# Channel attention then GLU on one core: first chunk's weights kept on chip, half of one batch's squares formed later, v's sums made by accumulating DMA

## The chip, the cores and the metric

The kernel runs on one core of one Trainium2 chip. The metric is the device time of one execution in microseconds, as the median of several runs. The engines named below are PE (matmuls), PEld (its weight loads), DVE (vector), ACT (scalar), POOL (GpSimd, here almost only the issuer of accumulating DMAs) and SP (the issuer of nearly all other DMAs).

## The reference, cut to what matters

Four batches (B = 4) of N = 6080 tokens with C = 256 channels pass through attention over channels and then through a gated layer. `q`, `k`, `v` are float32, the two weight matrices are float64.

```python
qn = q / (np.linalg.norm(q, axis=1, keepdims=True) + 1e-06)
kn = k / (np.linalg.norm(k, axis=1, keepdims=True) + 1e-06)
s = kn.transpose(0, 2, 1) @ qn / tau          # 256 x 256 for each batch
s = s - s.max(-1, keepdims=True)
a = np.exp(s)
a /= a.sum(-1, keepdims=True) + 1e-09
x = v @ a                                     # tokens x 256
h = x @ w_in                                  # d_ff = 2048
g = h * (1.0 / (1.0 + np.exp(-1.702 * h)))
out = g @ w_out
```

## The kernel before, in words

The attention matrix of a batch is multiplied into `w_in` once (`weights`, 8 units of 256 columns of d_ff each), so that the main part works straight on `v`: `g(v @ (a @ w_in)) @ w_out`. Both products of the main part are done by a 2x2 Strassen scheme with seven products (M1 to M7), in float32r with a high and a low part: three matmuls for one product (`three`).

The main part goes over the batches, in each over six chunks of 1024 tokens (the last has 960), in each over eight **pairs** (one unit of `w_in` and `w_out`). `front` forms the gated hidden values of a pair, `back` multiplies them with `w_out`. A pair's place counts from 0 over the whole program, 48 places to a batch. A chunk needs seven high-low tiles of `v` or of sums of its blocks; `values` makes them, in the order M5, M1, M2, M6, M7, M3, M4. Four of them need sums, which DVE adds in the kernel before.

What comes ahead for each batch:

- `Attention.unit`: scores (k transposed times q, summed over the tokens) from two row tiles at a time, 24 units to a batch, the last of 64 rows; and the squares of q and k for the norms: ACT squares, the sum goes into `acc`. For batches one and two (`b` = 0 and 1) the scores are float32 matmuls straight from the staged rows (`ps_s<-raw`), and DVE adds the squares. The rows come by `load_direct`, 1 MB (q and k) to a load, into staging buffers that are used again in turn. For batches three and four the rows are loaded unit by unit, split in high and low (`hl`), and an accumulating DMA from POOL (`acc<-raw`) adds the squares.
- `Attention.finish`, the softmax: column sums of `acc` (`ps_n`), roots on POOL (`rn`), scales spread by PE (`ps_b`), maximum and exponential, a transpose (`ps_t`), high and low part (`aT`).
- `weights`: the product `ps_w`, its Strassen sums (`wf`), high and low parts (`w`, stored in `w_d` for the later chunks).

The float64 weights are converted from their 32-bit words in the program: `win_convert` (loads `words<-in_w_in`, result stored in `win_d`) and `wout_convert` (`words<-in_w_out`, result with its sums stored in `wout_d`). In the kernel before, the first chunk reads both back from there: `wi<-win_d`, `wo<-wout_d`.

Each operation is a node with an engine, a cost, a due time and dependencies; a planner orders all nodes and the program is issued in this order. So every engine, and SP's and POOL's queues too, works through a fixed list in order, and an instruction that waits holds up all that stand behind it on its engine. The table that places the work ahead is `{1: (0, 6), 2: (19, 60), 3: (74, 118)}`: the scores of batch `b` are planned between these places (for batch two they come before place 0 already), the softmax from `end + 1`, the weights from `end + 4`, one unit to a place.

Of the kernel before, what the change touches and what calls it, by code (L numbers as in the profile page):

```python
# [20 lines left out]
P = 128  # L21
# [19 lines left out]
class Node:  # L41
    __slots__ = ("eng", "cost", "lag", "fn", "deps", "uses", "due", "idx", "start", "left", "ready", "outs")

    def __init__(self, eng, cost, fn, deps, uses, due, lag, idx):
        self.eng, self.cost, self.fn, self.due, self.lag, self.idx = eng, cost, fn, due, lag, idx
        self.deps = [d for d in deps if d is not None]
        self.uses = list(uses)
        self.start = None


class Plan:
# [27 lines left out]
    def graph(self):  # L79

        nodes = list(self.nodes)
        free_of = {}
        for n in self.nodes:
            deps = {id(d): d for d in n.deps}
            for b in n.uses:
                prev = b.prev
                while prev is not None and not prev.users:
                    prev = prev.prev
                if prev is not None:
                    r = free_of.get(id(prev))  # L90
                    if r is None:
                        r = Node(None, 0, None, prev.users, (), 0, 0, len(nodes))
                        free_of[id(prev)] = r
                        nodes.append(r)
                    deps[id(r)] = r
            n.deps = list(deps.values())
        ins, outs = [[] for _ in nodes], [[] for _ in nodes]
        for n in nodes:
            for d in n.deps:
                w = d.cost + d.lag  # L100
                if n.eng is not None and n.eng != d.eng:
                    w += self.DRAIN.get(d.eng, 0) + self.HOP + self.MARGIN.get(n.eng, 0)
                ins[n.idx].append((d.idx, w))
                outs[d.idx].append((n.idx, w))
        return nodes, ins, outs

# [84 lines left out]

VSUM = lambda b, c: False
QSUM = lambda b: b >= 2
HIACT = True
TURNED = True
TAILX = True
STQ = False
# [20 lines left out]
def channel_attention_then_glu(  # L218
# [61 lines left out]
    win_d = dr.tile([NPAIR, P, 2, NC2, 2 * P], F32, name="win_d")  # L280
    wout_d = dr.tile([NPAIR, P, 2, NA + 1, P], F32, name="wout_d")
    w_d = [dr.tile([NPAIR, P, 2, NA - 1, P], F32, name=f"w_d{i}") for i in range(B)]
# [141 lines left out]

    win_ready = {}

    def win_convert(grp, c, due, slot, lows, after=()):
# [7 lines left out]
        h = cast(lambda: hl()[:, 0], lambda: wf(), 4 * P, [n], [wf, hl], due + 0.7)  # L435
        l = low(lambda: hl()[:, 1], lambda: wf(), lambda: hl()[:, 0], 4 * P, [h], [wf, hl], due + 0.8)
        st = [
            load(
                lambda a=a: win_d[2 * grp + a, :, :, c, :],
                lambda a=a: hl()[:, :, a * 2 * P : (a + 1) * 2 * P], 256, [l], [hl], due + 1,  # L440
            )
            for a in range(2)
        ]
        for a in range(2):
            win_ready.setdefault(2 * grp + a, []).append(st[a])

    wout_ready = {}

    def wout_convert(u, due, slot, lows, after=()):
        raw = sbuf(slot, [P, 2, C, 2], U32, "words")  # L450
# [9 lines left out]
        h = cast(lambda: st()[:, 0], lambda: f(), 8 * P, [n], [f, st], due + 1)  # L460
        l = low(lambda: st()[:, 1], lambda: f(), lambda: st()[:, 0], 8 * P, [h], [f, st], due + 1.1)
        wout_ready[u] = load(lambda: wout_d[u], lambda: st(), 1024, [l], [st], due + 1.2)


    class Attention:
# [39 lines left out]
        def unit(self, u, due, after=()):  # L505
# [37 lines left out]
            for j in range(nt):  # L543
# [24 lines left out]
                news.append(n)  # L568
            if u == 0:
                self.acc_n = [g.add(  # L570
# [21 lines left out]
            else:  # L592
# [7 lines left out]
                    )  # L600
                ]

        def finish(self, slot):
# [128 lines left out]
    def weights(at, u, due, after=(), slot="Z", kept=None):  # L732

        wi = sbuf("wi", [P, 2, NC2, 2 * P], F32R, "wi")
        r = load(lambda: wi(), lambda: win_d[u], 512, [*win_ready[u], *after], [wi], due - 10)
        pb = bank(slot, "w")

        def fn():
            for i in range(NC2):
                ci = slice(i * P, (i + 1) * P)  # L740
                n = 0
                for l, m in ((0, 0), (0, 1), (1, 0)):
                    for j in range(NC2):
                        nc.tensor.matmul(  # L744
                            pb()[:, i * 2 * P : (i + 1) * 2 * P], lhsT=at.aT()[:, l, j, ci], rhs=wi()[:, m, j, :],
                            start=i == 0 and n == 0, stop=True, skip_group_check=True,
                        )
                        n += 1

        n = g.add("PE", 1440, fn, [at.a_h, at.a_l, r], [at.aT, wi, pb], due)  # L750
        f = sbuf(f"ra{u % 2}", [P, 8, P], F32, "wf")
# [368 lines left out]
    def fetch_wo(ck, p, u, due, after=()):  # L1120
        is_s = ck.kinds[p][2]
        cut = slice(1, 1 + NI) if is_s else slice(0, 4)

        def make(i):
            w = sbuf(f"wo{i}", [P, 2, NI, P], F32R, "wo")
            n = load(
                lambda: w()[:, :, : cut.stop - cut.start], lambda: wout_d[u, :, :, cut, :], 640,
                [wout_ready[u], *after], [w], due,
            )
            return w, n  # L1130

        return wo_slots.get((u, is_s), make)

    held = [None, {}]

    def fetch_wb(ck, p, pairs_of, due, after=()):
# [9 lines left out]
        if u not in places:  # L1146
            i = len(places)
            n = load(
                lambda: w()[:, i], lambda: wout_d[u, :, :, 1 + NI :, :], 256, [wout_ready[u], *after], [w], due,
            )  # L1150
            places[u] = n, i
# [32 lines left out]
    for u in range(2):  # L1184
        wout_convert(u, -55 + 4 * u, f"gi{u}", "oc1")
    nxt = Attention(1)
# [5 lines left out]
    for u in range(nu):  # L1192
        nxt.unit(u, -40 + 4.5 * u)


# [16 lines left out]
    def softmax_at(b, i):  # L1212
# [6 lines left out]
        return fn  # L1219

    def weights_at(b, u):
        return lambda t, here: weights(attention[b], u, t + 4, here)

    for b, (begin, end) in {1: (0, 6), 2: (19, 60), 3: (74, 118)}.items():
        if b >= 2:
            for u in range(nu):
                plan(begin + int(u * (end - begin) / nu), scores_at(b, u))
        for i in range(3):
# [6 lines left out]
    for b in range(B):  # L1235
        for s in range(total):
# [56 lines left out]
```

## Time and profile before

| | before |
|---|---|
| median of 3 runs | 2083.2 us (2081.8 to 2083.36) |
| profiled execution, its own time | 2082.57 us |
| its span, first to last instruction | 2080.8 us |
| PE busy | 2055.2 us (99%) |
| DVE busy | 1970.5 us (95%) |
| ACT busy | 1730.1 us (83%) |
| POOL busy | 110.6 us (5%) |
| DMA | 457.76 MB, mean 220 GB/s |
| mean granted TensorE clock | 0.999 of full speed |

The time stands 1.8 us over the span of the same execution, and the median of the runs 0.6 us over that execution's time. Busy time of PE counts a matmul from its start to its modelled end, so that a stretch in which matmuls follow closely is fully busy. The trace writes a float32 matmul of the direct scores as two records (`x8` for the four matmuls of a pair of row tiles).

### The profile page before, as it was taken

How to read it: one execution, taken by the hardware profiler on the slowest of the kernel's cores; microseconds unless marked ns; L12 is line 12 of the kernel's file. 1: busy time of each engine (PE TensorE's matmuls, PEld its weight loads, DVE VectorE, ACT ScalarE, POOL GpSimd, SP SyncE). 2: the span in 40 equal slices, each digit the busy share in tenths (PEclk: the TensorE clock that was granted, in tenths of full speed). 3: DMA queues.
4: the chain of work that ended last, by engine and by line, in shares of the span. 5: the costliest groups of instructions: out<-in, count | busy, mean ns of one | idle time of the engine just before them, and what ended most of it. 6: DMA issues, size and time to landing. Idle time of an engine off the chain costs nothing.

```text
span 2080.8 us, 27525 instructions
## 1 busy us (share of the span) xinstructions
PE 2055.2 (99%) x9556; PEld 1716.9 (83%) x9556; DVE 1970.5 (95%) x2457; ACT 1730.1 (83%) x2505; POOL 110.6 (5%) x127
## 2 busy tenths in 40 slices
PE   9899999999999999999999999999999999999999
PEld 8788888888888888888888888878888888888887
DVE  8997999999999999999999999999999999999898
ACT  6677888888888888888888888888888788888786
POOL 0000000010110100000000000010000000000000
PEclk9999999999999999999999999999999999999999
DMA  9986877778787666786777867648557555545545
GB/s 361 372 311 233 284 251 243 216 199 252 196 263 233 174 196 230 243 262 190 212 224 220 260 198 202 196 153 301 204 175 229 179 167 162 197 154 165 192 145 156
DMA packets 200314, 457.76 MB, mean 220 GB/s; under 512 B 17520, under 2 KB 87408, under 8 KB 199152
## 3 DMA queue, kind: packets, MB, share of 16 engines
q1 hardware_dynamic: 183072, 414.25, 57.2%
q0 software_dynamic: 17104, 41.75, 11.2%
q8 instruction: 76, 1.25, 0.2%
q14 instruction: 62, 0.51, 0.1%
HBM read 347.34 MB, written 66.85 MB: 199 GB/s over the span
## 4 chain that ended last, share of the span: by engine, by line
PE 74%; DVE 15%; ACT 4%; DMA 3%; issue 3%; SPq 0%; POOL 0%; DVEq 0%; ACTq 0%
PE ps_o L875 20%; PE ps_X L875 15%; PE ps_k L875 14%; PE ps_Z L875 10%; PE ps_Y L875 10%; DVE gp L312 3%; PE ps_s L558 3%; DVE gi L333 2%; DVE ga L312 2%; PE ps_w L744 2%; DVE acc L312 1%; DVE gr L333 1%; DVE gj L333 1%; DMA raw<-in_k 1%; ACT ga L902 1%
## 5 line engine op out<-in xcount | busy, mean ns | idle before, releaser
L875 PE MATMUL ps_X<-v,w 128*128 128x512 f32 (+1 forms) x1728 | 485.7, 389 | 2.1 <-ACT ps_Z L304 1.6
L875 PEld LDWEIGHTS ps_X<-v,w 128*128 128x128 f32 x1728 | 320.6, 188 | 70.3 <-ACT ps_Z L304 5.1
L333 DVE TENSOR_TENSOR gi<-ga,gi 128x1536 fp32r<-128x1536 f32 (+2 forms) x192 | 329.5, 1716 | 12.8 <-ACT gi L304 12.5
L902 ACT ACTIVATE ga<-ga 128x512 f32<-128x512 f32 (+1 forms) x384 | 238.7, 628 | 110.4 <-DVE ga L312 108.7
L875 PE MATMUL ps_Y<-v,w 128*128 128x512 f32 (+1 forms) x1152 | 324.7, 390 | 1.6 <-ACT ps_Y L304 1.6
L875 PE MATMUL ps_Z<-v,w 128*128 128x512 f32 (+1 forms) x1152 | 324.0, 389 | 1.0 <-ACT wf L304 0.5
L875 PE MATMUL ps_o<-gi,wo 128*128 128x512 f32 (+1 forms) x1200 | 322.4, 388 | 1.0 <-DVE oc L318 1.0
L875 PE MATMUL ps_o<-gj,wo 128*128 128x512 f32 (+1 forms) x1152 | 314.2, 388 | 1.5 <-DVE oc L312 1.0
L875 PE MATMUL ps_k<-gr,wb 128*128 128x512 f32 (+1 forms) x1104 | 293.2, 388 | 0.0
L304 ACT CAST gi<-ga 128x1536 fp32r<-128x1536 f32 (+2 forms) x192 | 279.1, 1454 | 4.7 <-PE ps_k L875 1.9
L875 PEld LDWEIGHTS ps_o<-gi,wo 128*128 128x128 f32 x1200 | 224.7, 188 | 47.1 <-DVE oc L318 1.8
L875 PEld LDWEIGHTS ps_Z<-v,w 128*128 128x128 f32 x1152 | 215.5, 188 | 46.3 <-ACT ps_Z L304 1.0
L875 PEld LDWEIGHTS ps_o<-gj,wo 128*128 128x128 f32 x1152 | 215.4, 188 | 45.1 <-DVE oc L312 1.4
L875 PEld LDWEIGHTS ps_Y<-v,w 128*128 128x128 f32 x1152 | 213.3, 188 | 47.5 <-ACT ps_Y L304 6.2
L875 PEld LDWEIGHTS ps_k<-gr,wb 128*128 128x128 f32 x1104 | 206.6, 188 | 41.0 <-DVE kb L312 0.2
L312 DVE TENSOR_TENSOR gp<-ga 128x1024 f32<-128x1024 f32 (+1 forms) x184 | 222.8, 1211 | 16.0 <-ACT ga L902 12.9
L333 DVE TENSOR_TENSOR gr<-gp,gr 128x1024 fp32r<-128x1024 f32 (+1 forms) x184 | 222.6, 1210 | 16.1 <-ACT gr L304 16.0
L333 DVE TENSOR_TENSOR gj<-gp,gj 128x1024 fp32r<-128x1024 f32 (+1 forms) x184 | 222.6, 1210 | 11.7 <-ACT gj L304 10.9
L304 ACT CAST gr<-gp 128x1024 fp32r<-128x1024 f32 (+1 forms) x184 | 191.5, 1041 | 30.1 <-DVE gp L312 27.5
L304 ACT CAST gj<-gp 128x1024 fp32r<-128x1024 f32 (+1 forms) x184 | 191.5, 1040 | 18.6 <-DVE gp L312 16.1
L875 PE MATMUL ps_k<-gi,wo 128*128 128x512 f32 (+1 forms) x552 | 155.0, 389 | 0.5 <-DMA wo<-wout_d 0.2
L304 ACT COPY ps_Y<-ps_X 128x512 f32<-128x512 f32 (+1 forms) x192 | 110.8, 577 | 31.3 <-PE ps_X L875 29.9
(127 smaller groups left out, 2721.6 us busy)
## 6 DMA issues: line engine op xcount, KB each, us to landing
w<-w_d SPq DMA_DIRECT2D x144, 768.0 KB, 5.0
wo<-wout_d SPq DMA_DIRECT2D x118, 640.0 KB, 5.2
wb<-wout_d SPq DMA_DIRECT2D x129, 256.0 KB, 4.1
acc<-raw POOLq DMA_DIRECT2D x44, 512.0 KB, 6.3
v_raw<-in_vT SPq DMA_DIRECT2D x20, 1024.0 KB, 7.7
out_T<-oc SPq DMA_DIRECT2D x80, 256.0 KB, 3.0
w<-w_d SPq DMA_DIRECT2D x144, 128.0 KB, 4.1
w_d<-wst SPq DMA_DIRECT2D x24, 768.0 KB, 5.2
```

Of the source, the lines that this page charges most:

```text
L304: return g.add("ACT", act(n, psum), lambda: nc.scalar.copy(dst(), src()), deps, uses, due)
L312: return g.add("DVE", dve(n), lambda: nc.vector.tensor_tensor(dst(), a(), b(), op=op), deps, uses, due)
L333: lambda: nc.vector.tensor_tensor(dst(), src(), hi().bitcast(F32), op=ALU.subtract),
L558: nc.tensor.matmul(out, lhsT=hl()[:pp, 1, j, l, ci], rhs=hl()[:pp, 0, j, r, :], start=begin and m == 0, stop=True, skip_group_check=True,)
L744: nc.tensor.matmul(pb()[:, i * 2 * P : (i + 1) * 2 * P], lhsT=at.aT()[:, l, j, ci], rhs=wi()[:, m, j, :], start=i == 0 and n == 0, stop=Tr ...
L875: nc.tensor.matmul(dst, lhsT=l(a), rhs=r(b), start=begin and n == 0, stop=True, skip_group_check=True,)
L902: lambda: nc.scalar.activation(dst(), src(), AF.Gelu_apprx_sigmoid, scale=sign), deps, uses, at,
```

## The change

Four things change, and with them the whole order that the planner makes.

- **First chunk's weights.** `win_convert` keeps both halves of a group (two units) in one `hl` buffer, and the first chunk's `ps_w` reads them there; `wi<-win_d` is gone for the first chunk, the store to `win_d` stays. `wout_convert` forms the four plain blocks of `w_out` right in the `wo` buffer from which the first chunk's `back` reads, and only the three further blocks that others need and the four sums are stored (896 KB in place of 1024 KB for a unit). It is called per unit, two pairs ahead, in place of two units at every second pair.
- **Squares of batch two.** Units 0 to 11 as before. For units 12 to 23 (`NQ = 12`) only the scores are formed early. `turn` copies `acc` and the scores to other buffers; `squares` loads the rows of those units again, at places 8 to 20, squares them on ACT and adds them by an accumulating DMA from POOL.
- **Places.** `SPANS = {1: (8, 20), 2: (31, 60), 3: (74, 118)}`: softmax and weights of batch two come 14 places later, and the scores of batch three start 12 places later and end where they did.
- **v's sums.** From batch two on (`VSUM`, 18 chunks) the four sums of `values` are made by DMA: a load of one block into `v_t` and accumulating DMAs from HBM for the others (`v_t<-in_vT`, `v_raw<-in_vT` on POOL). The branch stood in the kernel before, unused. M6's sum starts when M5's split is done, M4's when M6's is.

```diff
-VSUM = lambda b, c: False
+VSUM = lambda b, c: b >= 1
+NQ = 12
+SPANS = {1: (8, 20), 2: (31, 60), 3: (74, 118)}
...
-        hl = sbuf("hl", [P, 2, 4 * P], F32R, "cw")
...
+        if c == 0:
+            win_parts[grp] = (sbuf("hl", [P, NC2, 2, 4 * P], F32R, "cw"), [])
+        hl, done = win_parts[grp]
...
-        st = sbuf("hl", [P, 2, 8, P], F32R, "cs")
+        wo = sbuf(f"wo{i}", [P, 2, NI, P], F32R, "wo")
+        st = sbuf("wi", [P, 2, 4, P], F32R, "cs")
+        h = cast(lambda: wo()[:, 0, :4], lambda: f()[:, :4], 4 * P, [n], [f, wo], due + 0.7)
+        l = low(lambda: wo()[:, 1, :4], lambda: f()[:, :4], lambda: wo()[:, 0, :4], 4 * P, [h], [f, wo], due + 0.8)
         n = sums(f, [n], [f], due + 0.7)
...
+            load(lambda: wout_d[u, :, :, :3], lambda: wo()[:, :, 1:4], 384, [l], [wo], due + 1),
+            load(lambda: wout_d[u, :, :, 3:], lambda: st(), 512, [ls], [st], due + 1.2),
...
-            if u == 0:
+            if self.b == 1 and u >= NQ:
+                pass
+            elif u == 0:
...
+        def squares(self, u, due, after):
+            t0, nt, pp = self.units[u]
+            t = sbuf(f"ra{u % 2}", [P, 2, UT, C], F32, "raw")
...
+            n = g.add(
+                "ACT", act(2 * nt * C), lambda: nc.scalar.activation(both(), both(), AF.Square), ns, [t], due,
+            )
+            self.acc_n = [add_dma(lambda: acc()[:pp, :, :nt, :], both, [n, *self.acc_n], [t, acc], due + 1)]
...
-        wi = sbuf("wi", [P, 2, NC2, 2 * P], F32R, "wi")
-        r = load(lambda: wi(), lambda: win_d[u], 512, [*win_ready[u], *after], [wi], due - 10)
+        if kept:
+            wi, r = win_parts[u // 2]
...
+    if NQ < nu:
+        nxt.turn(-40 + 4.5 * nu)
...
-                for uu in (2 * grp, 2 * grp + 1):
-                    wout_convert(uu, t + 9 + 5 * (uu % 2), "vr", "oc1")
+            if b == c == 0 and u + 2 < NPAIR:
+                first_wo(u + 2, t + 9, "vr", "oc1")
```

How the order changes at three places that matter below. First SP's queue where the second half of the early loads of batch two stands. Before, from the load numbered `raw_481` to the sixth one, `raw_610` (1 MB with q and k; `words` are the float64 words, `wi` and `wo` the first chunk's weights read back):

```order
L292 DMA win_d<-cw 256x1x256 x2
L292 DMA raw_481<-in_k 128x1024
L292 DMA wi<-win_d 128x1024
L292 DMA raw_537<-in_q 128x1024
L292 DMA raw_537<-in_k 128x1024
L292 DMA words<-in_w_in 128x1024
L292 DMA wo<-wout_d 128x2x512 x2
L292 DMA win_d<-cw 256x1x256 x2
L292 DMA words<-in_w_out 128x512 x2
L292 DMA raw_610<-in_q 128x1024
L292 DMA raw_610<-in_k 128x1024
```

Of the change, the third to the sixth of the same loads (here `raw_385` to `raw_528`):

```order
L299 DMA raw_385<-in_q 128x1024
L299 DMA raw_385<-in_k 128x1024
L299 DMA raw_423<-in_q 128x1024
L299 DMA raw_423<-in_k 128x1024
L299 DMA win_d<-cw 256x1x256 x4
L299 DMA wout_d<-wo 256x1x384
L299 DMA wout_d<-cs 256x1x512
L299 DMA raw_498<-in_q 128x1024
L299 DMA raw_498<-in_k 128x1024
L299 DMA raw_528<-in_q 128x1024
L299 DMA raw_528<-in_k 128x1024
```

The reads of `wi` and `wo` and the next group's words no longer stand between these loads, and the words of further units come behind the sixth.

Second, DVE's list between the last sum of batch one's squares (`acc<-acc`) and the copy of the norms (`rn<-ps_n`), with which the softmax begins. Before, the last rows ahead of the copy (`cv` and `low` are a conversion of `w_in`, `v`, `v_t` and `v_raw` the first chunk's values; six more rows, five of these kinds and the low part of a unit of `w_out`, stand between `acc<-acc` and the first row here):

```order
L333 TENSOR_TENSOR v<-v_raw,v 128x512
L399 TENSOR_SCALAR low<-cv 128x512
L312 TENSOR_TENSOR v_raw<-v_t,v_raw 128x512
L404 SCALAR_TENSOR_TENSOR low<-words,low 128x512
L333 TENSOR_TENSOR v<-v_raw,v 128x512
L312 TENSOR_TENSOR v_raw<-v_raw 128x512
L333 TENSOR_TENSOR v<-v_raw,v 128x512 x3
L631 COPY rn<-ps_n 128x4
```

Of the change, all from `acc<-acc` on:

```order
L319 TENSOR_TENSOR acc<-acc 128x2x256
L319 TENSOR_TENSOR cf<-cf,low 128x512
L340 TENSOR_TENSOR cw<-cv,cw 128x512
L319 TENSOR_TENSOR cf<-cf 128x2x128
L340 TENSOR_TENSOR wo<-cf,wo 128x512
L680 COPY rn<-ps_n 128x4
```

Four conversions stand ahead of the copy in place of the first chunk's values, which now come behind it.

Third, POOL's queue in the second chunk of batch two, where v's sums for the next chunk are made (`ka`, `kb`, `kc` are sums of `back`, `acc` the last squares of batch three). Of the change:

```order
L334 DMA ka<-oc 128x512
L334 DMA acc<-raw 128x1024
L334 DMA kb<-oc 128x512
L334 DMA v_t<-in_vT 128x512
L334 DMA kc<-oc 128x512
L334 DMA acc<-raw 128x1024
L334 DMA acc<-raw 128x2x256
L334 DMA acc<-raw 64x2x256
L334 DMA v_t<-in_vT 128x512
L334 DMA v_raw<-in_vT 128x512
L334 DMA v_t<-in_vT 128x512
```

Before, no `v` row stood in POOL's queue; now four to a chunk stand among the others.

## Rows read from the trace of the kernel before

**Rows 1.** Page, head and part 1: span, then busy us (share) xinstructions by engine.

```profile
span 2080.8 us, 27525 instructions
PE 2055.2 (99%) x9556; PEld 1716.9 (83%) x9556; DVE 1970.5 (95%) x2457; ACT 1730.1 (83%) x2505; POOL 110.6 (5%) x127
```

**Rows 2.** Windows: stretch, length, busy us by engine, granted clock, DMA share, GB/s.

```profile
0.00:50.00 50.00, 46.51 (x212) 40.45 (x213) 40.45 (x55) 30.87 (x33) 0.70 (x6) 1.00 0.97 359
50.00:100.00 50.00, 41.71 (x217) 35.95 (x216) 49.46 (x97) 33.71 (x48) 2.09 (x1) 0.97 1.00 369
100.00:150.00 50.00, 49.28 (x234) 41.01 (x233) 49.73 (x82) 39.87 (x62) 0.00 (x0) 1.00 0.94 346
150.00:300.00 150.00, 149.05 (x715) 123.81 (x714) 134.09 (x202) 121.79 (x185) 3.81 (x4) 1.00 0.71 246
300.00:500.00 200.00, 199.13 (x943) 166.26 (x942) 195.08 (x228) 173.64 (x246) 14.82 (x17) 1.00 0.76 231
2000.00:2081.00 81.00, 76.01 (x348) 64.70 (x346) 70.64 (x83) 56.92 (x85) 2.59 (x3) 1.00 0.51 163
```

**Rows 3.** Waits of PE, whole span: us in total, times, longest.

```profile
PE ps_s L552 <- DMA raw<-in_k: 9.2, 6, 4.4
PE ps_X L875 <- ACT ps_Z L304: 1.6, 4, 0.6
PE ps_o L875 <- DVE oc L312: 1.0, 1, 1.0
```

**Rows 4.** Timeline of PE to the first chunk product: start us, us, instruction, [idle before].

```profile
1.06 3.78 PE L358 MATMUL ps_x<-ones 128*128 128x128 f32 x16 [1.06 <-DVE half L338]
4.63 1.74 PE L347 MATMUL ps_x<-ones 128*128 128x128 f32 x8
...
10.07 35.18 PE L552 MATMUL ps_s<-raw 128*128 128x256 f32 x160 [1.96 <-DMA raw<-in_k]
...
50.98 4.18 PE L358 MATMUL ps_x<-ones 128*128 128x128 f32 x36
55.00 0.95 PE L625 MATMUL ps_n<-ones,acc 128*128 128x1 f32 x8
...
64.81 0.68 PE L647 MATMUL ps_b<-x,ones 128*128 128x128 f32 x4 [1.37 <-DVE x L638]
...
73.90 0.60 PE L697 MATMUL ps_t<-ident,x 128*128 128x128 f32 x4
...
78.94 1.68 PE L744 MATMUL ps_w<-wi,aT 128*128 128x256 f32 x12
85.05 5.14 PE L552 MATMUL ps_s<-raw 128*128 128x256 f32 x16 [4.43 <-DMA raw<-in_k]
89.84 1.03 PE L875 MATMUL ps_Z<-v,w 128*128 128x512 f32 x3
90.71 0.86 PE L875 MATMUL ps_X<-v,w 128*128 128x512 f32 x3
```

**Rows 5.** Timeline of DVE, the same stretch.

```profile
51.99 0.67 DVE L312 TENSOR_TENSOR acc<-acc 128x512 f32<-128x512 f32 x1
...
61.61 0.15 DVE L631 COPY rn<-ps_n 128x4 f32<-128x4 f32 x1
```

**Rows 6.** Groups by line and shape: xcount | busy us, mean ns | idle before.

```profile
L312 DVE TENSOR_TENSOR v_raw<-v_raw 128x512 f32<-128x512 f32 x40 | 27.5, 688 | 0.2
L312 DVE TENSOR_TENSOR acc<-acc,raw 128x1024 f32<-128x1024 f32 x22 | 26.9, 1223 | 0.0
L581 ACT ACTIVATE raw<-raw 128x1024 f32<-128x1024 f32 x66 | 70.1, 1062 | 12.9 <-PE ps_s L552 10.2 <-DVE hl L333 2.4
```

**Rows 7.** DMA issues: xcount, KB each, median us from issue to landing.

```profile
acc<-raw POOLq DMA_DIRECT2D x44, 512.0 KB, 6.3
ka<-oc POOLq DMA_DIRECT2D x19, 256.0 KB, 6.4
```

**Rows 8.** Groups of POOL: its DMA issues, mean ns of one.

```profile
L327 POOL DMA_DIRECT2D acc<-raw x48 | 42.4, 883 | 618.0 <-ACT raw L581 430.7 <-PE ps_k L875 54.8 <-DMA wo<-wout_d 48.2
```

More of the change, by code (lines that the diff above doesn't have):

```diff
@@ L41 @@
 class Node:
-    __slots__ = ("eng", "cost", "lag", "fn", "deps", "uses", "due", "idx", "start", "left", "ready", "outs")
+    __slots__ = ("eng", "cost", "lag", "fn", "deps", "uses", "due", "idx", "start", "follows")
     def __init__(self, eng, cost, fn, deps, uses, due, lag, idx):
@@ L104, in graph @@
                 outs[d.idx].append((n.idx, w))
+            for d in n.follows:
+                ins[n.idx].append((d.idx, d.cost))
+                outs[d.idx].append((n.idx, d.cost))
         return nodes, ins, outs
@@ L433, in win_convert @@
         n = to_float32(wf, lows, raw, [r], due, False, wf)
[L434 to L436 removed]
+        if c == 0:
+            win_parts[grp] = (sbuf("hl", [P, NC2, 2, 4 * P], F32R, "cw"), [])
+        hl, done = win_parts[grp]
+        h = cast(lambda: hl()[:, c, 0], lambda: wf(), 4 * P, [n], [wf, hl], due + 0.7)
+        l = low(lambda: hl()[:, c, 1], lambda: wf(), lambda: hl()[:, c, 0], 4 * P, [h], [wf, hl], due + 0.8)
+        done.append(l)
         st = [
@@ L447, in channel_attention_then_glu, with wout_convert @@
     wout_ready = {}
-    def wout_convert(u, due, slot, lows, after=()):
+    def wout_convert(u, i, due, slot, lows, after=()):
         raw = sbuf(slot, [P, 2, C, 2], U32, "words")
@@ L601, in unit, with turn @@
                 ]
+        def turn(self, due):
+            old, S = self.acc, self.S
+            acc = sbuf("acc", [P, 2, UT, C], F32, "acc")
+            total = sbuf("ss", [P, HW], F32, "ss")
+            self.acc_n = [cast(lambda: acc(), lambda: old(), 2 * UT * C, self.acc_n, [old, acc], due)]
+            self.last = [cast(lambda: total(), lambda: S(), HW, self.last, [S, total], due + 0.1, psum=True)]
+            self.acc, self.S = acc, total
+        def squares(self, u, due, after):
+            t0, nt, pp = self.units[u]
+            t = sbuf(f"ra{u % 2}", [P, 2, UT, C], F32, "raw")
+            acc = self.acc
+            view = lambda i: t()[:pp, i, :nt, :]
+            ns = [
+                load(
+                    lambda i=i: view(i) if pp == P else view(i)[:, 0], lambda i=i: self.rows(i, t0, nt, pp), 128 * nt,
+                    after, [t], due - 10, 7000,
+                )
+                for i in range(2)
+            ]
+            both = lambda: t()[:pp, :, :nt, :]
+            n = g.add(
+                "ACT", act(2 * nt * C), lambda: nc.scalar.activation(both(), both(), AF.Square), ns, [t], due,
+            )
+            self.acc_n = [add_dma(lambda: acc()[:pp, :, :nt, :], both, [n, *self.acc_n], [t, acc], due + 1)]
         def finish(self, slot):
@@ L732, in weights @@
     def weights(at, u, due, after=(), slot="Z", kept=None):
-        wi = sbuf("wi", [P, 2, NC2, 2 * P], F32R, "wi")
-        r = load(lambda: wi(), lambda: win_d[u], 512, [*win_ready[u], *after], [wi], due - 10)
+        if kept:
+            wi, r = win_parts[u // 2]
+            part = lambda m, j: wi()[:, j, m, u % 2 * 2 * P : (u % 2 + 1) * 2 * P]
+        else:
+            wi = sbuf("wi", [P, 2, NC2, 2 * P], F32R, "wi")
+            r = [load(lambda: wi(), lambda: win_d[u], 512, [*win_ready[u], *after], [wi], due - 10)]
+            part = lambda m, j: wi()[:, m, j, :]
         pb = bank(slot, "w")
@@ L748, in fn @@
                         n += 1
-        n = g.add("PE", 1440, fn, [at.a_h, at.a_l, r], [at.aT, wi, pb], due)
+        n = g.add("PE", 1440, fn, [at.a_h, at.a_l, *r], [at.aT, wi, pb], due)
         f = sbuf(f"ra{u % 2}", [P, 8, P], F32, "wf")
@@ L1120, in fetch_wo, with first_wo @@
     def fetch_wo(ck, p, u, due, after=()):
-        is_s = ck.kinds[p][2]
-        cut = slice(1, 1 + NI) if is_s else slice(0, 4)
         def make(i):
+            assert ck.kinds[p][2]
             w = sbuf(f"wo{i}", [P, 2, NI, P], F32R, "wo")
[L1126 to L1129, printed above, removed]
+            n = load(lambda: w(), lambda: wout_d[u, :, :, :NI, :], 640, [*wout_ready[u], *after], [w], due)
             return w, n
-        return wo_slots.get((u, is_s), make)
+        return wo_slots.get((u, ck.kinds[p][2]), make)
+    def first_wo(u, *args):
+        wo_slots.get((u, False), lambda i: wout_convert(u, i, *args))
     held = [None, {}]
@@ L1148, in fetch_wb @@
             n = load(
-                lambda: w()[:, i], lambda: wout_d[u, :, :, 1 + NI :, :], 256, [wout_ready[u], *after], [w], due,
+                lambda: w()[:, i], lambda: wout_d[u, :, :, NI:, :], 256, [wout_ready[u][1], *after], [w], due,
             )
@@ L1219, in softmax_at, with squares_at @@
         return fn
+    def squares_at(u):
+        return lambda t, here: attention[1].squares(u, t + 6, here)
     def weights_at(b, u):
         return lambda t, here: weights(attention[b], u, t + 4, here)
[L1224 to L1227, printed above, removed]
+    for b, (begin, end) in SPANS.items():
+        for u in range(NQ if b == 1 else 0, nu):
+            at_ = begin + int((u - NQ) * (end - begin) / (nu - NQ)) if b == 1 else begin + int(u * (end - begin) / nu)
+            plan(at_, squares_at(u) if b == 1 else scores_at(b, u))
         for i in range(3):
```

17 lines of the change are left out of this document (10 added, 7 removed).

## The prediction

> **What bounds the kernel now.** I read the head of the page first: PE is busy 2055.2 of 2080.8 us, DVE 1970.5 [rows 1]. Only 25.6 us of PE's span are idle, and the change takes no matmul away (9,310 in the program before and after), so what can be won is those 25.6 us and little else. Where they lie is read from the windows [rows 2]: 3.5 us in the first 50, 8.3 us in the next 50, and 5.0 in the last 81, where the tail of the last chunk stands and the change touches nothing. Between 100 and 2000 us that leaves 25.6 - 3.5 - 8.3 - 5.0 = 8.8 us in 1900. In the first 100 us the DMA engines are busy 97% and 100% of the time at 359 and 369 GB/s, and DVE in the second 50 for 49.46 us. The list of waits agrees: the longest entry is the direct scores waiting for rows, 9.2 us in six waits, and no other entry is over 1.6 us [rows 3]. So the place to cost is the start, up to the first product of the first chunk at 89.84 us [rows 4].
>
> **The start, as a sum.** Ahead of that product PE has to do (all [rows 4]) two warming groups of 3.78 and 1.74, one of 4.18, the norms 0.95, `ps_b` 0.68, `ps_t` 0.60, `ps_w` 1.68, together 13.6 us, and direct scores at 35.18 / 160 = 0.220 us a record. Before, 144 score matmuls (288 records) stand ahead of it, 63.4 us; with the start at 1.06 that makes 78.1, and 89.84 is 11.8 later. In the changed order 142 stand ahead (284 records, 62.5 us): PE alone would be there at 77.1.
>
> Does DMA allow it? Counted along SP's queue to the sixth early load of batch two, before: 18.7 MB of rows and 11.5 MB of other transfers, at 364 GB/s (the mean of the first two windows, [rows 2]) 83 us, and the last scores ahead of the product start at 85.05 after a wait of 4.43 for exactly that load [rows 4]. After the change: the same 18.7 MB, but 5.6 MB of others, 67 us. The reads of `wi` and `wo` (1.6 MB by then) are gone, and the words of further units stand behind. DMA stops being the limit by some 10 us.
>
> Does the softmax chain allow it? It begins with the norms. Before, `ps_n` is over at 55.95, but the copy `rn` starts only at 61.61, though the last sum of squares was over at 52.66 [rows 4, 5]: DVE works through its list, and the first chunk's values stand ahead of the copy. In the changed list four conversions stand there (three of 512 columns at about 0.69 a piece, one of 256), some 2.2 us, and PE does `ps_n` ahead of its warming group. From 52.66 that is 54.9 to 55.0 for the copy, 6.6 us sooner. From the copy to the product the chain took 28.2 us (61.61 to 89.84). Eight adds of squares stand on DVE in that stretch before, five after: 3 x 1.2 = 3.6 us less [rows 6]; the other rows are about as many. 55.0 + 24.6 = 79.6. PE also waited 1.96 us at 10.07 for the second load [rows 4], ahead of whose second half words of `w_in` stood; now only rows stand there, and batch one's scores may end up to 2 us sooner: 77.6 to 79.6. I take 78.5 for the product, 11.3 us sooner. Two matmuls more are left for later, 0.9 us: the term is **-10.4 us**. Its bounds: -5.7 if only the copy comes sooner (6.6 - 0.9), -11.8 if PE loses nothing.
>
> **The first pairs.** DVE is busy 49.73 us of 50 from 100 to 150 [rows 2], so pairs that start 11 us sooner need as much of DVE's work gone. Eleven adds of batch two, 128x1024 at 1.22, are: 13.5 us [rows 6]. That covers it with some 2 us over; if the cover falls short, PE waits by as much. I take 0, bounds 0 to +3. Each return from direct scores to chunk products costs 1.03 - 0.86 = 0.17 us [rows 4]; after the first product there are three more of them in the new order: **+0.5 us**.
>
> **The squares formed later.** Twelve units cost one square of 1.06 each on ACT [rows 6], 12.7 us, moved from a stretch where ACT is busy 33.71 or 39.87 of 50 into 150 to 300, where it is busy 121.79 of 150 [rows 2]. The eight weight units of batch two leave that stretch in exchange. Hidden, at 0, while ACT keeps some 10% idle; if it doesn't, up to +12.7. Each square waits for a load, and the gates of the pair behind it on ACT wait with it; what they do not produce PE lacks next. `turn` adds two copies on ACT (1024 and 512 columns), under 2 us there. Softmax and weights of batch two are ready at place 31 and wanted at 48: seventeen pairs of about 10 us hide them.
>
> **Batch three's scores** come in 29 places rather than 41, 0.83 units a pair rather than 0.59. DVE has 195.08 of 200 us from 300 to 500 already [rows 2]; 0.24 units of about 1.9 us (a low part and a sum) add 0.46 us to a pair of some 10 us, and the dense part starts where v's sums are still on DVE. I take **+1**, bounds 0 to +4.
>
> **v's sums.** 18 chunks of four additions, 72 at 0.69 [rows 6], take 49 us from DVE, which PE waits for directly only in small pieces (the longest entry 1.0, [rows 3]). Of the 8.8 us of idle time in the middle I let it win **-1**, bounds 0 to -6. In exchange DMAs must land in time. Nothing in the trace adds from HBM into SBUF; the nearest rows are the adds between buffers: 6.3 and 6.4 us to landing after an issue of 0.88 [rows 7, 8]. M6's sum is the tight one: M5's low part (0.69), the issue, the landing, 8.0 us. In ACT's new order 13 to 19 instructions stand between M5's and M6's cast; at ACT's mean of 1730.1 / 2505 = 0.69 [rows 1] that is 9 to 13 us. M4's sum has twice that. So I take 0, with 1 to 5 us in hand.
>
> The Trainium skill (SBUF — State Buffer, section "SBUF: two separate sides") speaks against this part: while DVE runs a float32 instruction in the mode that takes both ports, GpSimd cannot write the descriptors of its DMAs, and it reports one going from about 620 to 3100 ns so. By that figure M6's sum would take 2.5 us more, 10.5, which is over the short gaps, and with a microsecond lost in each chunk the sum would be 18 us higher. The trace shows POOL's issues at a mean of 883 ns next to a DVE that is 95% busy [rows 1, 8], so here it does not show.
>
> Sum: -10.4 + 0.5 + 1 - 1 = -9.9. From the profiled execution's 2082.57 that is 2072.7; the median of the runs shown is 0.6 higher, so **2073**.
>
> **Rivals.**
> - *DVE's relief counts for more* (0.12): less load on DVE takes most of the 8.8 us in the middle as well. For it: DVE is the engine behind most small waits. Against: these are pieces under 1.6 us spread over 24 chunks [rows 3]. 2073 - 6 = 2067.
> - *The start is given back* (0.17): the chain or DVE, not DMA, holds the product, or the pairs after it wait for DVE, or ACT runs short from 150 to 300. For it: DVE is as full as DMA there [rows 2]. With only -5.7 at the start and +3 to +7 behind: 2080 to 2085, no change that can be told.
> - *v's sums come late* (0.11), slower: if issue and landing of M6's sum take over 9 us rather than 7.3 beside busier DMA queues, ACT's cast waits, all casts and gates behind it wait, and PE after them. It decides from 0.8 us a chunk (14.4 us in 18 chunks, which eats the gain and 4 more); at 1 to 2 us a chunk 2091 to 2109.
> - The forecast itself has 0.60.
>
> **How the numbers follow.** About 0.2% (4.2 us) is what a measurement can tell here from no change. Faster by more are the forecast and the first rival, 0.72; the same 0.17, slower 0.11. The forecast's own range is 2068 to 2079: the start's bounds (-5.7 to -11.8) with the small terms. The range for 8 in 10 goes from 2065 to 2086: it takes in the second rival and leaves out the third.
>
> **What would show it.** Right: the first chunk product at 77 to 80 us, no `wi<-win_d` ahead of it, the wait for rows down from 9.2 to under 3 us, `rn` copied near 55; PE's idle time between 50 and 100 us down from 8.3 to under 2; DVE's busy time down by about 60 us without PE noticing; POOL's DMAs of `v_t` landing in 4 to 7 us. Wrong: `ACT v` or `ACT raw` waiting for DMA in the list of waits with more than 10 us in total and PE behind them, a DVE that is full from 80 to 150 us with PE's products waiting for `gi` or `ga`, or more than 10 us of idle time on PE between 100 and 2000.

## The result and the profile after

| | before | after |
|---|---|---|
| median, timed side by side | 2081.80 us (2080.54 to 2083.36) | 2092.16 us (2089.16 to 2099.73) |
| ratio | | 1.0057, 95% interval 1.0035 to 1.0079 |
| profiled execution, its own time | 2082.57 us | 2092.16 us |

Slower by 10.4 us, outside the range and on the other side of no change. The head of the page, the two large DMA queues (MB, share of 16 engines' span; q1 is SP's, q0 POOL's accumulating DMAs) and the chain that ended last:

```profile
span 2090.4 us, 27784 instructions
...
PE 2061.0 (99%) x9556; PEld 1715.4 (82%) x9556; DVE 1927.6 (92%) x2380; ACT 1734.3 (83%) x2517; POOL 182.3 (9%) x212
...
q1 hardware_dynamic: 189152, 415.65, 58.0%
q0 software_dynamic: 29472, 66.60, 18.3%
...
PE 72%; DVE 14%; DMA 6%; ACT 5%; issue 2%; SPq 0%; DVEq 0%; ACTq 0%
```

Against [rows 1] DVE has 77 instructions and 42.9 us of work less, and PE gained nothing from it. The same matmuls show 5.8 us more busy time (some 5 of it are longer distances between the starts of matmuls, too short to show as gaps) and 29.4 us idle where there were 25.6. The same two queues before:

```profile
q1 hardware_dynamic: 183072, 414.25, 57.2%
q0 software_dynamic: 17104, 41.75, 11.2%
```

SP's queue moves about what it moved: the first chunk's part alone takes 9.4 MB off it (e4 below, 404.81), and the reloads for the late squares and the first blocks for v's sums (4.7 MB) put as much back. POOL's has 24.85 MB more (18.7 of v's sums, 6.2 of late squares) and takes 7.1 points more of the engines' time. A megabyte costs the engines 18.3 / 66.60 = 0.27% there and 58.0 / 415.65 = 0.14% on SP's: twice as much.

Where PE stands still is read from the windows after, which answer to [rows 2] (columns as there: PE, PEld, DVE, ACT, POOL, clock, DMA share, GB/s):

```profile
0.00:50.00 50.00, 48.30 (x222) 42.32 (x222) 37.96 (x48) 29.58 (x32) 0.70 (x6) 1.00 0.94 344
50.00:100.00 50.00, 49.48 (x263) 42.75 (x263) 49.66 (x98) 38.09 (x59) 1.04 (x1) 1.00 0.94 333
100.00:150.00 50.00, 50.00 (x240) 42.50 (x239) 46.84 (x92) 35.11 (x59) 0.00 (x0) 1.00 0.81 285
150.00:300.00 150.00, 147.21 (x650) 119.02 (x649) 135.91 (x175) 128.90 (x192) 13.45 (x15) 1.00 0.88 266
300.00:500.00 200.00, 197.24 (x943) 162.94 (x942) 191.67 (x246) 170.10 (x247) 11.95 (x13) 1.00 0.76 238
500.00:1000.00 500.00, 487.63 (x2324) 407.79 (x2323) 464.46 (x559) 425.02 (x611) 57.84 (x66) 1.00 0.83 241
1000.00:1500.00 500.00, 496.19 (x2339) 414.59 (x2338) 465.44 (x559) 425.55 (x618) 53.91 (x61) 1.00 0.79 231
```

and from the stretch with the largest loss in the kernel before:

```profile
500.00:1000.00 500.00, 496.99 (x2352) 416.60 (x2351) 481.37 (x587) 430.90 (x621) 34.52 (x38) 1.00 0.72 221
```

The first 100 us hold 97.78 us of PE's work instead of 88.22, 9.6 more: the start came as forecast. From 500 to 1000, where most of the dense scores of batch three (29 places instead of 41) and the first of v's sums lie, 9.4 us of it are gone again, with the DMA engines at 83% in place of 72%; the rest of 100 to 2000 loses some 4 more. The start in PE's timeline after, beside [rows 4]:

```profile
49.50 0.95 PE L674 MATMUL ps_n<-ones,acc 128*128 128x1 f32 x8
50.31 4.26 PE L365 MATMUL ps_x<-ones 128*128 128x128 f32 x36
...
64.36 0.60 PE L746 MATMUL ps_t<-ident,x 128*128 128x128 f32 x4
...
68.06 1.77 PE L798 MATMUL ps_w<-cw,aT 128*128 128x256 f32 x12
69.67 7.07 PE L571 MATMUL ps_s<-raw 128*128 128x256 f32 x32
76.39 1.04 PE L929 MATMUL ps_Z<-v,w 128*128 128x512 f32 x3
```

The first product stands at 76.39, 13.5 us sooner; in DVE's timeline `rn` is copied at 51.02. What is new stands in the lists of waits (us in total, times, longest), PE's:

```profile
PE ps_o L929 <- DVE oc L319: 4.5, 4, 2.3
PE ps_t L746 <- ACT ga L956: 3.9, 2, 3.4
PE ps_k L929 <- DVE gi L340: 3.1, 3, 1.7
PE ps_Z L929 <- ACT wf L311: 2.5, 3, 1.9
```

and those of DVE and ACT for DMA:

```profile
DVE oc L319 <- DMA out_T<-oc: 11.5, 7, 3.4
...
ACT wst L821 <- DMA w_d<-wst: 7.9, 4, 4.1
...
ACT sq L602 <- DMA raw<-in_k: 7.1, 6, 2.3
...
ACT hl L311 <- DMA raw<-in_k: 4.3, 2, 2.4
```

Before, the first of these was 1.8 us. `oc` is the pair of buffers from which the output is stored: DVE may write one again when its store has landed. The same stores in the list of DMA issues (KB each, median us to landing), before and after:

```profile
out_T<-oc SPq DMA_DIRECT2D x80, 256.0 KB, 3.0
```

```profile
acc<-raw POOLq DMA_DIRECT2D x55, 512.0 KB, 7.2
...
out_T<-oc SPq DMA_DIRECT2D x80, 256.0 KB, 4.6
...
v_t<-in_vT POOLq DMA_DIRECT2D x45, 256.0 KB, 5.6
```

A plain store that the change doesn't touch takes half as long again. One case in the chain of work from 975 to 995 us of the kernel after (start us, us, what):

```profile
981.29 1.13 DVE gp L319
982.42 0.61 DVE oc L325
983.04 0.02 issue
983.05 9.79 DMA out_T<-oc
992.85 0.02 issue
992.87 0.70 DVE oc L319
993.57 0.04 issue
993.62 1.62 PE ps_o L929 x3
```

DVE stands still for a store that lands after 9.79 us, and PE's `ps_o` waits 2.3 us for the buffer that DVE would have emptied.

Right behind this wait PE also runs slower. The three matmuls of `ps_o` in the last row take 1.62 us and the three behind them 1.48, where three elsewhere take 0.84. The granted clock of 994 to 997 us is 0.50 of full speed, the lower level of 1.2 GHz. Groups of three usually start 0.68 us apart; here twelve matmuls fill 4.45 us instead of 2.7. The kernel before has such a stretch in its start: PE is busy 0.63 of the 4 us from 80 to 84, the granted clock from 84 to 88 is 0.57, and 16 score records take 5.14 us [rows 4] where 0.220 a record would give 3.5.

### The profile page after: what moved, and what is told of

Its sections match the earlier page's. It is cut to its first block, busy times and chain, and to the rows that moved or that the text cites. A ratio compares the mean times of both kernels' runs of the same rounds, so it can differ in the third digit from the quotient of the medians.

```text
span 2090.4 us, 27784 instructions
## 1 busy us (share of the span) xinstructions
PE 2061.0 (99%) x9556; PEld 1715.4 (82%) x9556; DVE 1927.6 (92%) x2380; ACT 1734.3 (83%) x2517; POOL 182.3 (9%) x212
## 3 DMA queue, kind: packets, MB, share of 16 engines
q1 hardware_dynamic: 189152, 415.65, 58.0%
q0 software_dynamic: 29472, 66.60, 18.3%
## 4 chain that ended last, share of the span: by engine, by line
PE 72%; DVE 14%; DMA 6%; ACT 5%; issue 2%; SPq 0%; DVEq 0%; ACTq 0%
PE ps_o L929 19%; PE ps_X L929 14%; PE ps_k L929 14%; PE ps_Z L929 10%; PE ps_Y L929 10%; DVE gp L319 3%; PE ps_s L577 3%; DMA raw<-in_k 3%; DVE gi L340 2%; DMA out_T<-oc 2%; PE ps_w L798 1%; DVE ga L319 1%; DVE gr L340 1%; DMA w_d<-wst 1%; DVE acc L319 1%
```

## The experiments

Three theories. **A:** the accumulating DMAs load the DMA engines, all transfers land later, and work that waits for a buffer or a row makes PE wait, far from the sums themselves. **B:** the new order is a worse one, whatever its DMAs move. **C:** batch three's scores stand too dense in their fewer places. "Dense" below means 29 places for them, "wide" 41. "Against before" is the difference of the medians timed side by side; the change itself stands at +10.4. An interval of a ratio is some +-2 us wide, that of the change +-4.5, so a difference to the change has some +-5, and one of two other runs some +-3; a smaller one can't be told from nothing.

| run | median us | ratio to before, 95% | against before |
|---|---|---|---|
| e1, v's adds narrow | 2084.32 | 1.0007 (0.9998 to 1.0016) | +2.1 |
| e2, v's sums on DVE | 2077.51 | 0.9976 (0.9967 to 0.9986) | -4.7 |
| e3, scores wide | 2082.12 | 1.0001 (0.9993 to 1.001) | -0.1 |
| e4, first chunk only | 2073.60 | 0.9957 (0.9944 to 0.9969) | -8.6 |
| e5, first chunk and v | 2077.25 | 0.9966 (0.9954 to 0.9979) | -5.1 |
| e6, all adds narrow | 2074.84 | 0.9968 (0.9955 to 0.998) | -7.5 |
| e7, other order | 2084.73 | 1.0013 (1.0004 to 1.0022) | +2.4 |
| e8, wide, v on DVE | 2074.35 | 0.9967 (0.9957 to 0.9977) | -8.0 |
| e9, stores narrow | 2088.81 | 1.0029 (1.0018 to 1.004) | +5.0 |
| e10, e4 with adds narrow | 2072.31 | 0.9946 (0.9932 to 0.9959) | -11.5 |
| e11, v's adds plain | 2088.13 | 1.003 (1.0019 to 1.004) | +5.8 |
| e12, all adds plain | 2077.79 | 0.9978 (0.9969 to 0.9987) | -4.5 |

**e1 and e6: the changed kernel in its own order, with less to accumulate.**

```diff
-            p1 = add_dma(P1, lambda: rows(0, 1), [p1], [vt], due - 32)
+            few = lambda f: (lambda: f()[:, :P]); p1 = add_dma(few(P1), few(lambda: rows(0, 1)), [p1], [vt], due - 32)
...
-            self.acc_n = [add_dma(lambda: acc()[:pp, :, :nt, :], both, [n, *self.acc_n], [t, acc], due + 1)]
+            self.acc_n = [add_dma(lambda: acc()[:pp, :1, :1, :], lambda: both()[:, :1, :1], [n, *self.acc_n], [t, acc], due + 1)]
```

The first edit is e1's, for all four sums alike; e6 has both, and a like one for the squares of batches three and four, a quarter of their columns.

> The changed kernel with the four accumulating DMAs of v's sums cut to their first 128 of 512 columns (the sums of the other columns are left out). The order of every engine and queue is the same, and so are all waits; only the bytes that these DMAs move are a quarter. Theory A (the added DMA load makes output stores, w_d stores and row loads land late, and DVE and ACT wait for them): most of the loss goes, 2074 to 2082, landings of out_T back towards 3 us, the DVE wait for out_T under 4 us. Theory B (the new order is a less lucky one, its waits stand whatever the DMA load): 2089 to 2094. Theory C (batch three's scores in fewer places are too dense): 2089 to 2094 too, with the waits for raw rows unchanged.

> The changed kernel in its own order, with v's accumulating DMAs and also those of all squares cut to a quarter of their bytes (the rest of these sums is left out). Theory A carried through (every accumulating DMA loads the engines alike): 5 to 8 us under the run with only v's cut, 2076 to 2079. Theory B: the rest of the loss is the order's, 2082 to 2085, with the wait of ps_t (3.9 us) still there.

e1 brings 8.3 us back for 14.0 MB, e6 17.9 for 36.2 MB, instruction for instruction in the order of the change; B and C, which give nothing there, fall as the whole cause. A's numbers miss on both sides: e1 lies 2 us above its bracket, with DVE's wait for `out_T` at 8.5 us and not under 4, and e6 comes 9.5 us under e1 instead of 5 to 8. Of e6's 36.2 MB, 17.7 are squares of batches three and four, which the kernel before accumulates too; what they cost in another order is e10's question. In e6 `DVE oc` waits 2.5 us for its stores, and PE for `oc` 0.6. What stays in e6 is a part of B: `ps_t` still waits 3.4 us at once. ACT's timeline of the kernel after shows why (start us, us, instruction): batch three's softmax alternates with the gates, and each change of function loads a table, four in 8.4 us.

```profile
771.42 1.28 ACT L714 ACT_TABLE_LOAD   x1
...
773.33 1.28 ACT L956 ACT_TABLE_LOAD   x1
...
775.24 1.28 ACT L714 ACT_TABLE_LOAD   x1
...
778.52 1.28 ACT L956 ACT_TABLE_LOAD   x1
```

`ps_t` starts at 780.46, when the gate behind the fourth load is through. The change loads ten tables in all, the kernel before eight, and e7's order eight too, where `ps_t` waits 1.0 us.

**e11 and e12: the same bytes in the same order, without the addition.** The DMA of v's sums (e11), and of the squares too (e12), writes plainly; sums then hold only what came last.

```diff
-    def add_dma(dst, more, deps, uses, due):
-
+    def add_dma(dst, more, deps, uses, due, plain=False):
+        how = {} if plain else {"accum_op": ALU.add}
...
-            "POOL", 1200, lambda: nc.gpsimd.dma_start(dst(), more(), accum_op=ALU.add), deps, uses, due, lag=ALAG,
+            "POOL", 1200, lambda: nc.gpsimd.dma_start(dst(), more(), **how), deps, uses, due, lag=ALAG,
...
-            p1 = add_dma(P1, lambda: rows(0, 1), [p1], [vt], due - 32)
+            p1 = add_dma(P1, lambda: rows(0, 1), [p1], [vt], due - 32, plain=True)
```

The other three of v's sums, and in e12 the squares, get `plain=True` alike; the sums of `back` go on accumulating.

> The changed kernel in its own order on every engine and queue; v's 72 accumulating DMAs write plainly, the same bytes from the same places to the same places, but without the addition (so v's sums hold only the block that came last). Theory A (it is the load on the DMA engines that costs, and an accumulating byte loads them about twice as much as a plain one, 18.3% for 66.60 MB against 58.0% for 415.65 MB): the share of that queue falls by some 2.5 to 3 points, about half of the engine time of these 18.6 MB goes, and a little under half of what the narrow v sums brought comes back (8.3 us for three quarters of it, 11 for all): 3 to 6 us, 2086 to 2089. A rival within it: only the bytes and their queue count, whatever they do, then no change, 2090 to 2093. The other rival: only the addition costs, then 9 us or more come back, 2083 or less. Theory B, the order: 2090 to 2093.

> As the run with v's DMAs written plainly, and the squares' accumulating DMAs written plainly too (the sums of squares hold only the unit that came last). About 48 of the 66.60 MB accumulate no more. Theory A: half of what the run with all adds narrow brought, taken for all bytes and not three quarters of them (17.9 us there): 10 to 13 us come back, 2079 to 2083. Only bytes: 2090 to 2093. Only the addition: 2075 or less. Theory B: 2090 to 2093.

e11 brings back 4.6 us, in A's bracket, though by its interval that is not clear of nothing; e12 14.9, which is, and more than its 10 to 13. POOL's queue and the stretch from 500 to 1000 us in e12:

```profile
q0 software_dynamic: 23808, 66.60, 11.4%
```

```profile
500.00:1000.00 500.00, 493.86 (x2362) 414.59 (x2361) 471.50 (x567) 432.20 (x620) 42.96 (x67) 1.00 0.74 245
```

The 66.60 MB now take 11.4% of the engines, about what the 41.75 MB took before, the DMA share is 74% instead of 83%, more is moved (245 against 241 GB/s), PE works 6.2 us more in the stretch, and DVE's wait for `out_T` falls from 11.5 to 0.7 us. So it is not the bytes on POOL's queue as such, but the engine time that goes with adding them.

Two things change along with the addition: POOL is busy 138.9 us and not 182.3, and its queue has 23,808 packets and not 29,472. e1 leaves both as they were (182.4 and 29,472) and cuts bytes alone; there the share falls from 18.3% to 14.9% for 14.0 MB, 0.24% a megabyte. So most of the price goes with the accumulated bytes. And what the stores gain is not their median landing, which falls from 4.6 to 4.3 us only, but the latest ones: from 500 to 1000 the slowest took 9.9 us in the change and 7.6 in e12.

**e9: the stores of the output cut to a quarter of their columns**, the rest as in the change.

```diff
-            (load if ck.end else store)(lambda: outT[rows, at : at + hw], lambda: v()[:, :hw], 256, [op], [s], t + 3)
+            (load if ck.end else store)(lambda: outT[rows, at : at + hw // 4], lambda: v()[:, : hw // 4], 256, [op], [s], t + 3)
```

> The changed kernel in its own order on every engine, but each store of the output writes 128 of its 512 columns (three quarters of the output is left unwritten); 18.7 MB less to write, no accumulating DMA touched. Theory A (the added accumulating DMAs delay everything in the queues, and PE loses where a buffer waits for its store): these 18.7 MB are plain writes, so they relieve the DMA engines by less than the 14.2 MB of accumulates in the run with narrow v sums, but the stores themselves land sooner, and the 11.5 us that DVE waited for them go to under 4; 3 to 6 us come back, 2086 to 2089. If the wait for these stores were the whole loss, 10 us or more come back, under 2082. Theory B (the order alone costs): 2090 to 2093.

2088.81 lies in A's bracket (5.4 us back, hardly more than the interval), but one of its numbers is a miss: DVE's wait for these stores falls only to 9.1 us, not under 4. The landing of all 96 stores (min, median, max), after and e9:

```profile
DMA to landing us min/median/max: 2.0/4.7/9.9
```

```profile
DMA to landing us min/median/max: 1.5/4.1/9.4
```

A quarter of the bytes, in as many packets, lands 0.6 us sooner, while the whole store landed 1.8 us sooner in the kernel before (2.9). Most of what the stores lost is thus not their own bytes' time; that it is the time of what lies ahead of them on the engines fits this and is not shown apart. Taking bytes off the stores is no remedy for their wait.

**e2, e3, e4, e5 and e8: the parts of the change apart.** `VSUM = lambda b, c: False` puts v's sums back on DVE (e2, e4, e8); batch three's scores get their 41 places back in e3 and e8, at the price that the last scores end 12 places later; e4 and e5 have the first chunk's weights in the new way, but squares and places as before.

```diff
-SPANS = {1: (8, 20), 2: (31, 60), 3: (74, 118)}
+SPANS = {1: (8, 20), 2: (31, 72), 3: (86, 130)}
```

That was e3 and e8; e4 and e5 have

```diff
-NQ = 12
-SPANS = {1: (8, 20), 2: (31, 60), 3: (74, 118)}
+NQ = 25
+SPANS = {1: (0, 6), 2: (19, 60), 3: (74, 118)}
```

> The changed kernel with v's sums on DVE as before (VSUM off), the other parts as changed; the planner makes a new order. Theory A: the added DMA load goes altogether and the start's gain of some 12 us stays: 2070 to 2080, with DVE busy 1975 us again. Theory B: anywhere from 2075 to 2095. Theory C: 2088 or more, since the scores stay dense and DVE has 49 us more to do.

> The changed kernel with the scores of batch three at places 31 to 72 and of batch four at 86 to 130, as many places each as in the kernel before (41 and 44), so that they are not denser than there; a new order. Theory C: the losses between 300 and 1000 us go, 2076 to 2083. Theory A: the load of v's sums stays, 2086 to 2093, with late landings now at other times. Theory B: anywhere from 2080 to 2098.

> The first part alone: the first chunk's weights read where they are formed; all squares early, v's sums on DVE, places as before; a new order. Theories A and C: no added DMA load and no denser scores, so what the start gains stays. Of the start's 12.5 us the squares' part is missing (DVE has 13 us more to do there), so 5 to 10 us better than before: 2072 to 2077. Theory B: 2074 to 2090.

> The first chunk's part and v's sums by DMA; all squares early and the places as before. Theory A (v's accumulating DMAs make other transfers land late): 7 to 12 us over the first part alone (2073.6), 2081 to 2086, with DVE waiting for out_T 5 us or more. Theory B (it was only that order): 2071 to 2076, since DVE has 49 us less to do.

> First chunk's part and late squares, scores of batches three and four at 31 to 72 and 86 to 130, v's sums on DVE. If the density of batch three's scores costs the 3.9 us by which the late squares stand over the first part alone: 2073 to 2075. If the late squares themselves cost it (reloads and adds between places 8 and 20): 2076 to 2079.

Each of these runs has an order of its own. The times of e2, e4 and e8 came as expected. e3 is a miss for A (2086 to 2093) and lies in C's bracket; e5 lies under A's 2081 to 2086, with DVE's wait for `out_T` at 3.2 us and not 5 or more, and over B's 2076.

From the medians, v's sums by DMA cost 3.5 us on the first chunk's part alone (e5 less e4), 7.9 with wide scores (e3 less e8), 15.1 with dense ones (the change less e2). Dense scores cost 3.3 without v's sums (e2 less e8) and 10.5 with them. In these orders each is small alone and dear beside the other; e7 shows how far that holds. The stretch from 500 to 1000 us of e2 (dense, no v's sums) and of e3 (v's sums, wide):

```profile
500.00:1000.00 500.00, 498.67 (x2389) 418.25 (x2388) 484.70 (x593) 431.02 (x622) 39.05 (x44) 1.00 0.77 232
```

```profile
500.00:1000.00 500.00, 497.76 (x2355) 416.92 (x2354) 470.57 (x566) 430.50 (x622) 54.45 (x62) 1.00 0.80 237
```

With either alone PE is idle 1.3 and 2.2 us there; with both 12.4. The late squares, with their places, cost nothing that can be told: e8 is 0.6 us from e4. In the windows that is a gain and a loss: PE is busy 3.2 us more from 100 to 300 in e8 than in e4 (198.11 against 194.96) and 5.2 less from 300 to 500 (194.56 against 199.74), where the softmax of batch two now stands. e4, the first chunk's part alone, and e8 are the fastest with the full computation. Part of e4's gain is the clock: the mean granted clock of its runs is 0.999 to 1.000, of the change's 0.996 to 0.999, and the kernel before, timed beside e4, has a mean of 0.998. A difference of 0.002 is 4 us of 2082, an estimate from these clocks; the change has lost them again.

**e7: the same work in another order**, by a planner's constant for the latency of accumulating DMAs (`ALAG = 8800` for 9000).

> The changed kernel with the planner's allowance for an accumulating DMA at 8800 rather than 9000 ns: the same work and the same DMA bytes in another order. Theory A: 2086 to 2096, as the load stays. Theory B: away from 2092 by more than 6 us, most likely lower (2078 to 2086).

Its stretch from 500 to 1000:

```profile
500.00:1000.00 500.00, 491.34 (x2331) 409.90 (x2330) 463.60 (x559) 424.15 (x610) 57.53 (x65) 0.99 0.82 240
```

It lies 8.0 us under the change with the same bytes and the same parts, under A's bracket and inside B's; from 500 to 1000 PE works 491.34 us rather than 487.63. The stores land no sooner: a median of 5.1 us, in e5 4.9 and in e3 4.8, where the change has 4.6. But DVE waits 2.4, 3.2 and 7.0 us for them, not 11.5. So the order decides which late landing meets a wait, and the change's is the worse of the two tried. Even e7's loses the start's gain whole: +2.4 against before.

With e7 in the change's place v's sums cost 7.1 us beside dense scores (less e2) and dense scores 2.5 beside v's sums (less e3), and both together 10.4 (less e8), no more than the 7.9 and 3.3 that they cost apart. That the two make each other dearer is seen in the change's order alone.

**e10: e4 with the adds of the squares cut to 256 of their 1024 columns** (the sums of squares stay incomplete). Its expectation speaks of one element a partition and some 24 MB; the edit leaves a quarter, 128 KB of 512 an add.

```diff
-self.acc_n = [add_dma(a, sqv, [s, *self.acc_n], [sq, acc], due + 1.5)]
+self.acc_n = [add_dma(lambda: a()[:, :1, :1], lambda: sqv()[:, :1, :1], [s, *self.acc_n], [sq, acc], due + 1.5)]
```

> The first chunk's part alone in its own order, with the accumulating DMAs of the squares of batches three and four cut to one element a partition (the sums of squares are left incomplete). Theory A in the form that a megabyte of accumulates costs more the fuller the DMA engines are: here they are at 73% in the stretch from 500 to 1000 us and stores land in 3.0 us, so little comes back, 0 to 2 us, 2071.5 to 2073.6. If a megabyte costs the 0.43 us of the run with all adds narrow whatever the load, some 24 MB give 10 us, 2063. Theory B: the order is the same, no change, 2073 to 2074.

2072.31 lies in A's range. 2.9 us come back against before for 17.7 MB, 0.16 us a megabyte, no more than the intervals let pass for nothing. In the change the first 14.0 MB cut (e1) were worth 0.59 us each, the next 22.2 (e6 less e1) 0.43. So an accumulated megabyte looks dearer where the engines are fuller and the order has less slack; which of the two counts for how much, these runs don't part.

## Why the prediction was wrong

- **The start, right.** Forecast 78.5 for the first product, measured 76.39, 0.7 ahead even of the 77.1 that was worked out for PE alone (rows of PE overlap by some tenths at their ends, so their sum is a little too long). The norms came at 49.50, before at 55.00 [rows 4], and the copy `rn` at 51.02 rather than the 55 forecast: the squares were through sooner, too. The wait for rows fell from 9.2 [rows 3] to 1.0 us. e4 alone gains 8.6, near the -10.4 of the term; DMA stopped being the limit, as counted. The clock was no term of the sum: the slow stretch from 84 to 88 us lay inside the 11.8 us that the kernel before lost there, and with PE's pause it went.
- **The first pairs (0) and the squares formed later (0), right in the sum.** PE is busy all of 100 to 150. The next two stretches are idle 1.8 and 1.9 us more than in [rows 2]; e8 less e4 puts the late squares, with all that moved for them, at +0.6 in the end, not to be told from 0. A batch has 25 units, the 24th with one row tile and the 25th with 64 rows, so thirteen squares move and not twelve; the term stays as small.
- **Batch three's scores (+1, bounds 0 to +4), inside the bounds alone and outside them beside v's sums in the change's order:** 3.3 and 10.5 us; 2.5 in e7's. They were costed by DVE's time; what they make dense is also the loads and accumulating DMAs of the rows.
- **v's sums (-1, bounds 0 to -6): the step that failed.** It asked whether the sums land in time. They do: `v_t` lands after 5.6 us, ACT's casts wait 0.4 us for a DMA of `v`, and the third rival with its place at M6's cast did not happen; that the measured 2092.16 lies within its 2091 to 2109 is chance. What was left out of the sum is the engine time that 18.7 MB of accumulating DMA take from all other transfers. In the change's own order, three quarters of these bytes were worth 8.3 us (e1). Between orders, in place of -1 stand +3.5, +7.1, +7.9 or +15.1. The numbers lay ready: POOL's queue before took 11.2% for 41.75 MB and SP's 57.2% for 414.25, and one wait of 1.8 us of DVE for a store told how little slack `oc` had.
- **DVE's relief.** The fall was 42.9 us, not 60, and v's sums have 33 of it (e2's 1960.9 less the change's 1927.6) instead of 49. DVE's rows follow each other 0.60 us apart where each is 0.68 long, so count times duration is too much; that makes 43, and where the other 10 went is open. That the relief buys PE anything is not shown: no run with v's sums on DMA is faster than its fellow without. e12, with the relief and with the addition gone from some 49 MB, is still 5.4 us over the forecast, of which the wait of `ps_t` behind the table loads is 3.4.
- **What would show it.** "More than 10 us of idle time on PE between 100 and 2000" was the sign that came: 22.3 us by the windows. The place was not among those that I named, `ACT v` and `ACT raw`, but `DVE oc`, `ACT wst`, `ACT sq`.
- **GpSimd's descriptors.** The Trainium skill (SBUF — State Buffer, section "SBUF: two separate sides") says that GpSimd cannot write its DMAs' descriptors while DVE runs an instruction in a mode that takes both ports. The 54 issues of `v_t` took 850 to 1222 ns, median 867, beside a DVE that is busy 92%, so no such wait shows here; which of DVE's instructions ran in that mode, the trace does not tell. That the 18 us of the prediction's sentence on it come near the 19 by which the forecast was missed is chance.

Shown by the runs: the loss falls by 14.9 us when the same bytes go in the same order without the addition; half of the bytes written plainly are squares of batches three and four, which the kernel before accumulates too. Shown as well: another order of the same work is 8.0 us faster. Argued only: how the last 5 us of e12 split between table loads and other places of the order. Not tried: e7's order without the additions, the change with only the late squares narrow, and a third `oc` buffer.

## What to carry to other kernels

Work that is moved from an engine to DMA is paid for on the DMA engines: take its share of their time from the queue's own row (here twice as much per megabyte for accumulating DMA), add it to the share of the stretch where it lands (here 72% became 83%), and look there for every buffer that is freed by a landing. Time a change that remakes the order in a second order before its parts are priced: the two parts that cost 3 and 8 us apart cost 18 together in one order and 10 in another. And if the engine that is relieved was not the one that PE waits for, expect little on the other side of the sum.

## What the runs showed of the hardware

- The addition in a DMA costs time of the DMA engines, not only POOL's: 18.3% of 16 engines for 66.60 MB with it, 11.4% for the same bytes when some 49 MB of them were written plainly (e12).
- Beside this traffic a store's landing depended little on its size: 256 KB 4.7 us, a quarter of it in as many packets 4.1 (medians, e9), while between the kernel before and the change it went from 2.9 to 4.7.
- PE's clock fell to its lower level (0.50 of full speed, 1.2 GHz) right behind a pause of 2.3 us, and twelve matmuls took 4.45 us instead of 2.7 (994 to 997 us of the change).
